# An S4D convolution block with a feed-forward: where the start of the kernel stores spectra, adds the skip weights and forms the modulation

## The chip, the cores and the metric

The kernel runs on one core of one Trainium2 chip. A core has TensorE (PE, with its weight loads PEld), VectorE (DVE), ScalarE (ACT), GpSimd (POOL) and SyncE (SP), which share an on-chip memory, and 16 DMA engines between that memory and DRAM. Every engine works through its own row of instructions in order; semaphores hold it back until what it reads is there. DMA transfers are issued by an engine (here SP, POOL and ACT) onto a queue of its own. The metric is the device time of one launch, in microseconds (us).

## The reference, cut to what matters

```python
def S4D(u):                                # u: (1, 2048, 576); D = 576 channels, N = 128 states
    dt = exp(log_dt);  A = -exp(log_A_real) + 1j * A_imag;  C = (C_real + 1j * C_imag) * dt
    K = 2 * einsum("dn,dnl->dl", C, exp(A * dt * pos)).real       # a kernel of 2048 taps a channel
    y = irfft(rfft(u, 4096) * rfft(K, 4096))[:2048]               # a causal convolution
    return y + u * D_skip
sa, ca, ga, sb, cb, gb = split(silu(c) @ w_mod, 6)                # modulation rows, 576 each
h = layernorm(x) * (1 + ca) + sa
x = x + ga * S4D(h)
h = layernorm(x) * (1 + cb) + sb
x = x + gb * (relu(h @ w1) @ w2)                                  # 576 -> 4608 -> 576
```

All inputs and the output are fp32. `y + u * D_skip` is the same as adding `D_skip` to tap 0 of each channel's kernel K, which is how both kernels do it.

## The kernel before

The 2048 rows are four blocks of 512. The S4D kernel has 2048 taps too, in four pieces; the convolution is done block against piece, in the frequency domain, with the transforms written as matmuls (`transform`, `transform1`, `inverse`) and sums and differences on DVE (`butterfly`). Block s needs the spectra U of blocks 0 to s and the spectra of the kernel pieces. `Ud` and `Rd` in DRAM keep such spectra for the later blocks. The channels go through in two halves, p = 0 and p = 1 (so U_0_0, K_0_1 and so on, the block first). The feed-forward of a block follows its convolution; the convolution of the next block, and the rest of the S4D kernel, are spread in small steps over the feed-forward ahead.

*The S4D kernel's first piece.* `KGen.first` makes it in six groups of 96 channels. A group consists of angles (`turns`: `ph` on PE from `zt` and `zr`, then fractions on DVE), exponentials and sines (ACT: `E`, `s`, `c`, `Zp`, `zs`), products of them on DVE and POOL (the factors `W1` and `W2`, each computed by doubling), and matmuls `kps <- W, W` that multiply the factors out (`products`). ACT copies a group's taps from PSUM to the table `ke` (`rows`, line 351); after three groups, that is half of the channels, `store` (line 446) writes `ke` to `kd` in DRAM with two DMAs, and `load_kt` reads it back in another layout as the tile `kt`, on SP's queue for block 0. The half 0 is stored at 110 us and loaded at 128, the half 1 at 176.6 and 179.7. `zs` are spectra of the generator (called `Zd` in DRAM, two stores a group, line 349) which the feed-forward loads back when it makes the rest of the kernel.

*Before the first group.* `KGen.setup` makes the rates: first `turn` and `rate` for parts[0], and then `turn` for the two other parts (ten DVE instructions with `ai`, `th`, `zt`), exponentials on ACT, and `rate` for them (`lar`, `zr`), then `cc`. `mod` makes the first three modulation rows: silu of `c` (ACT `ex`, DVE `ex`, its reciprocal, `ct`, and `cb`, the columns spread out), fifty matmuls for each row (`mod_products`), and the row's spreading over the partitions. The order of the `next(...)` calls in `KGen.first` (lines 377 to 395) is the order on the engines; nothing reorders it.

*From the last group to the feed-forward.* `first` stops inside the sixth group, and `main` runs the convolution of block 0 in the order of its generator: the transform of the kernel's half 0 (`mm_K(0)`, PE `ps_f` at 147.9), of the block's halves (`mm_U`), the last group's products (`late`) and `rows` with its store, the load of `kt` for half 1, the last three modulation rows (`mod_late`: the same matmuls for `sb`, `cb`, `gb`, two transposes each for `sb` and `cb`), the butterflies of U_0_0, U_0_1 and K_0_0 on DVE, and the transform of the kernel's half 1 (`transform1`, PE `ps_f` at 186.7). A save of a spectrum to DRAM (`save`, line 840) is a DMA issued by POOL, 1152 KB each.

*The skip weights* are added with `skip` (line 1258), on one partition and 288 elements of `kt`, after the load: for the half 0 on DVE (called in `early`, line 639), for the half 1 on POOL (called in `mm_K`). The skip weights lie in partition 0 of the tile `m_gb` and come with one DMA at the start.

Of the kernel before, what the change touches and what calls it, by code (L numbers as in the profile page):

```python
# [18 lines left out]
P = 128  # L19
# [4 lines left out]
NB = 4  # L24
NF = F // P
G = 96
# [23 lines left out]
class KGen:  # L50
# [31 lines left out]
    def setup(self, I):  # L82


        nc, pc = self.nc, self.pc
        kept = self.tc.keep_in_program_order
        tmp = lambda n: self.pw.tile([KR, NH, P], F32, tag="W2", bufs=5, name=n)
        lar, ai = tmp("lar"), tmp("ai")
        dtT = pc.tile([KR, NH], F32, name="dtT")
        lv = pc.tile([KR, NS], F32, name="lv")  # L90
        dt = self.pc.tile([P, D], F32, tag="T0", bufs=2, name="dt")
        self.cc = self.pa.tile([P, 2, D], F32, name="cc")
        self.halfpi = pc.tile([P, 1], F32, name="halfpi")
# [12 lines left out]
        z = self.zz = [self.pa.tile([KR, NH, P], F32R, name=f"z{n}") for n in "tr"]  # L106

        def split(zx, src, h):
            if h.start == 0:
                self.act(zx[:, h], src, AF.Copy)  # L110
            else:
                kept(nc.vector.tensor_copy(zx[:, h], src))
            self.v(zx[64:, h], src[64:], zx[64:, h], ALU.subtract)

        def turn(h):
            th = self.pc.tile([KR, 4, P], F32, tag="T1", bufs=2, name="th")
            dtb = dtT[:, h].unsqueeze(2).broadcast_to([KR, 4, P])
# [12 lines left out]
        self.diag(lv, slice(0, 8))  # L130
        turn(parts[0])
        self.diag(lv, slice(16, 25))
        self.diag(lv, slice(32, NS))
        yield
        rate(parts[0])
        yield
        self.diag(lv, slice(8, 16))
        self.diag(lv, slice(25, 32))
        yield
        for h in parts[1:]:  # L140
            turn(h)
        self.act(lar[:, 4:], lar[:, 4:], AF.Exp)
        self.act(dt, dt, AF.Exp)
        for h in parts[1:]:
            rate(h)
        for r in range(2):
            self.stt(
                self.cc[:, r], self.cc[:, r], 2.0 - 4.0 * r, dt, op0=ALU.mult, op1=ALU.mult
            )
        yield  # L150
# [111 lines left out]
    def powers(self, g, e, f):  # L262

        Z = self.ps.tile([P, 2, 512], F32, tag="Z", name=f"Zp_{g}")[:, :, 0 : 4 * G]
        Z = Z.rearrange("p r (i c) -> p r i c", c=G)
        zs = self.pc.tile([P, 2, 2, G], F32, tag="zs", bufs=2, name=f"zs_{g}")
        by_u = lambda x: x.rearrange("p i (u c) -> p u i c", u=2)
        c = self.abs(f)
        self.act(by_u(Z[:, 1]), f[:, :, 0:4], AF.Sin, scale=-TWO_PI)
        self.act(by_u(zs[:, :, 1]), f[:, :, 4:6], AF.Sin, scale=-TWO_PI)  # L270
        self.cos(by_u(Z[:, 0]), c[:, :, 0:4])
        self.cos(by_u(zs[:, :, 0]), c[:, :, 4:6])
        for r in (1, 0):
            self.pool(by_u(zs[:, :, r]), by_u(zs[:, :, r]), e[:, :, 4:6], op=ALU.mult)
        self.Z[g] = Z, zs

        def moduli():
            for r in (1, 0):
                self.v(by_u(Z[:, r]), by_u(Z[:, r]), e[:, :, 0:4], ALU.mult)

        return moduli
# [42 lines left out]
    def first(self, setup, mod):  # L324
# [8 lines left out]
        def sines(g):  # L333
# [12 lines left out]
            self.moduli = self.powers(g, E[4], F[2])  # L346
            zs = self.Z[g][1]
            for u in range(2):
                nc.sync.dma_start(out=k.Zd[2 * g + u], in_=zs[:, :, :, u * H : u * H + H])

        def rows(g):
            qs = slice(24 * (g % 3), 24 * (g % 3) + 24)
            self.act(ke[:, :, qs], ps[g].rearrange("p q a -> p a q"), AF.Copy)
            if g % 3 == 2:
                self.store(0, g // 3, ke.rearrange("p a q -> p (a q)"), nc.sync)

        def save(g):
# [26 lines left out]
        some(turns, 2)  # L384
        next(setup)
        run(turns, self.exps(0))
        next(mod)
        next(setup)
        next(mod)
# [182 lines left out]
class Body:  # L572
# [3 lines left out]
    def build(self):  # L576
        nc, tc, I = self.nc, self.tc, self.I
        with ExitStack() as ctx:
# [15 lines left out]
            self.x2, self.xT, self.ended = {}, {}, -1  # L594
            self.sm = self.pool(ctx, "sm")
            self.gb = self.sm.tile([P, D], F32, name="m_gb")
            self.dsk = self.gb[0:1]
            nc.gpsimd.dma_start(out=self.dsk, in_=I["dsk"].unsqueeze(0))
            self.x2p = [self.pool(ctx, "x2a")]
            kg = KGen(self)  # L600
            with ExitStack() as c2:
# [5 lines left out]
    def early(self, kg):  # L607
# [28 lines left out]
            ))  # L636
        yield
        self.kt0 = kg.kt0
        kept(self.skip(self.kt0, 0, nc.vector))
        for i in (0, 2, 1, 3):  # L640
            kept(nc.vector.tensor_tensor(h[:, i], h[:, i], self.m["ca"], op=ALU.mult))
            kept(nc.vector.tensor_tensor(h[:, i], h[:, i], self.m["sa"], op=ALU.add))
# [93 lines left out]
    def mod_late(self):  # L736


        nc, act, cb = self.nc, self.nc.scalar.activation, self.cb
        for j, nm in ((3, "sb"), (4, "cb"), (5, "gb")):  # L740
            self.mod_weights(self.wm[nm], slice(j * D, (j + 1) * D), nc.sync)
        for nm in ("sb", "cb", "gb"):
            yield
            w = self.wm[nm]
            ps = self.cps.tile([P, 512], F32, tag="cps", bufs=self.nps, name=f"mps_{nm}")
            self.mod_products(ps, cb, w, nc.tensor.matmul)
            row = self.cv.tile([P, 2 * P], F32, tag="row", bufs=1, name=f"row_{nm}")
            act(row[:, 0:P], ps[:, 0:P], AF.Copy)
            for o in (P, P + 64):
                act(row[0:32, o : o + 64], ps[0:32, P : P + 64], AF.Copy)  # L750
            if nm == "gb":
                yield
                self.mod_spread(row, self.md[nm], self.m[nm], Kept(self.tc, nc.gpsimd))
                return
            ps = self.cps.tile([P, 512], F32, tag="cps", bufs=self.nps, name=f"mpt_{nm}")
            nc.tensor.transpose(ps[:, 0:P], row[:, 0:P], self.ident)
            nc.tensor.transpose(ps[:, P : P + 32], row[0:32, P:], self.ident[:32, :32])
            act(
                self.m[nm], ps[:, 0 : 5 * 32].rearrange("p (j r) -> p j r", r=32)[:, :, 0],
                AF.Copy, bias=1.0 if nm == "cb" else 0.0,  # L760
            )

    def pool(self, ctx, name, **kw):
        return ctx.enter_context(
# [172 lines left out]
    def conv(self, s):  # L937
# [31 lines left out]

        def mm_K(p, Z):  # L970
            ktv = kt[p].rearrange("p (t dd g) q -> p t dd g q", t=2, g=2)
            if s == 0 and p == 1:
                self.skip(kt[p], p, Kept(self.tc, nc.gpsimd))
            src = lambda n2: ktv[:, n2 // 2, :, n2 % 2]
            if s == 0 and p == 1:
                return self.transform1(src, self.fcK, self.fcKn, Z)
            return self.transform(src, self.fcK, Z, s == 0)

        def spec_U(p, Z):
            U = self.spec(f"U_{s}_{p}")  # L980
            yield from self.butterfly(Z, U, -1)
            yield -1
            if s + 1 < NB or p == 1:
                self.save(self.Ud[s][p], U)
            Us.append(U if s == 0 or p == 0 else None)

# [86 lines left out]
        if s == 0:  # L1073
# [14 lines left out]
            yield from spec_K(0, ZK)  # L1088
            ZK = self.spec("Z")
            yield from mm_K(1, ZK)  # L1090
            self.save(self.Rd[0][0], Ks[0], Kept(self.tc, nc.gpsimd))
        else:
            yield from both(self.norm1(x2, h), mm_K(0, ZK))
            kt[1] = kernel_tile(1)
# [156 lines left out]
    def load_kt(self, kt, s, p, eng):  # L1251
# [2 lines left out]
            out=kt,  # L1254
            in_=bass.AP(tensor=kd.tensor, offset=kd.offset, ap=[[72, P], [9216, 16], [1, 72]]),
        )

    def skip(self, kt, p, eng):
        k0 = kt.rearrange("p (t dd g) q -> p t dd g q", t=2, g=2)[0:1, 0, :, 0]
        dv = self.dsk.rearrange("o (dd p q) -> o dd p q", dd=4, p=2)[:, :, p]  # L1260
        return eng.tensor_tensor(k0, k0, dv, op=ALU.add)

    def ffn(self, gens):

# [311 lines left out]
def _layout(inputs):  # L1576
# [14 lines left out]
    r["dsk"] = a["A_D_skip"]  # L1591
# [44 lines left out]
```

## Time and profile before

| | us |
|---|---|
| median of three runs | 1326.09 (1322.65, 1326.09, 1332.2) |
| the profiled execution | 1328.0 |
| its span, first to last instruction | 1326.2 |
| mean granted PE clock, as a share of full speed | 0.943 |

Busy over the whole span: PE 1212.6 us (91%), DVE 895.2 (67%), ACT 494.3 (37%), POOL 160.3 (12%). The feed-forward's first matmul comes at 228.7 us (`hps`, line 1330). The stretch ahead of it is what the change edits. There DVE is the engine with the most work.

| stretch, us | what runs | PE busy | DVE busy | PE clock | DMA GB/s |
|---|---|---|---|---|---|
| 0 to 23 | loads, first angles, first exponentials | 6.7 | 9.4 | 1.00 | 263 |
| 23 to 36 | turns, rates, first modulation rows | 9.1 | 12.4 | 1.00 | 230 |
| 36 to 140 | six groups of the kernel | 63.7 | 96.1 | 0.56 | 256 |
| 140 to 162 | transforms of kernel half 0 and of x | 16.2 | 21.7 | 0.77 | 302 |
| 162 to 187 | last group, its store and load, modulation | 14.9 | 23.9 | 0.73 | 313 |
| 187 to 229 | transform of half 1, product, inverse, norm | 30.7 | 32.9 | 0.84 | 142 |

Read such a table with the engines' waits beside it: an engine that is idle costs time only if the work that ends last stands behind it.

### The profile page before, as it was taken

To read this page: it belongs to the slowest core of one execution; us is meant where nothing else is said; L and a number is where in the kernel's file an instruction comes from. 1 tells how busy PE (TensorE), PEld (TensorE's weight loads), DVE (VectorE), ACT (ScalarE), POOL (GpSimd) and SP (SyncE) were. 2 spreads that over 40 slices of the span, in tenths; PEclk is the share of its full clock that TensorE was granted. 3 is DMA by queue.
4 is the path that set the end of the run, shared out by engine and by line. 5 is a ranking of instruction groups with operands and counts; after the bars stand their busy time and mean duration, and the time that the engine had idled before them with its cause. 6 is when DMAs were issued, how large, how long until landed. Compare 5 with 4: busy or idle time off the path is not lost.

```text
span 1326.2 us, 25994 instructions
## 1 busy us (share of the span) xinstructions
PE 1212.6 (91%) x10720; PEld 960.7 (72%) x10720; DVE 895.2 (67%) x1324; ACT 494.3 (37%) x863; POOL 160.3 (12%) x256
## 2 busy tenths in 40 slices
PE   4566676899989999999999999999999999999998
PEld 3344554677767787777777887887888888888886
DVE  5989988999986999689468994457996222111112
ACT  5677623222223422622243225433323353223231
POOL 0756511011000100100001000100000000000000
PEclk9556777999989999999999999999999999999999
DMA  8567882889878967799779995867996667666652
GB/s 273 210 235 294 300 314 80 345 298 333 311 259 302 342 223 278 247 403 343 262 270 339 351 340 159 285 205 285 346 395 189 173 177 230 195 202 191 200 178 70
DMA packets 122635, 345.85 MB, mean 261 GB/s; under 512 B 23916, under 2 KB 24212, under 8 KB 111764
## 3 DMA queue, kind: packets, MB, share of 16 engines
q1 hardware_dynamic: 105940, 228.14, 51.8%
q0 software_dynamic: 16064, 114.67, 23.0%
q8 instruction: 84, 1.38, 0.4%
q10 hardware_dynamic: 512, 1.38, 0.3%
q14 instruction: 35, 0.29, 0.1%
HBM read 262.73 MB, written 81.40 MB: 259 GB/s over the span
## 4 chain that ended last, share of the span: by engine, by line
PE 70%; DVE 17%; DMA 6%; issue 4%; ACT 2%; POOL 1%; SPq 0%; ACTq 0%; DVEq 0%; POOLq 0%
PE hps L1330 28%; PE acc L1356 28%; PE ps_f L850 5%; DMA L1d<-w 3%; PE kps L71 2%; PE ph L71 2%; DVE W1r L484 2%; DVE T L482 2%; PE ps_i L1057 2%; PE kps L517 1%; DVE w L1300 1%; DMA x<-in_x_dram 1%; DVE W1r L486 1%; DVE W1r L488 1%; DVE w L1312 1%
## 5 line engine op out<-in xcount | busy, mean ns | idle before, releaser
L1330 PE MATMUL hps<-xh,w 128*128 128x512 f32 x1152 | 395.7, 404 | 0.7 <-ACT xh L47 0.7
L1356 PE MATMUL acc<-w,hh 128*128 128x512 f32 x1136 | 362.1, 401 | 3.7 <-ACT hh L1335 3.5
L1336 DVE SCALAR_TENSOR_TENSOR hl<-hps,hh 128x512 fp32r<-128x512 f32 x144 | 99.4, 690 | 309.2 <-ACT hh L1335 308.5
L1330 PEld LDWEIGHTS hps<-xh,w 128*128 128x128 f32 x1152 | 219.0, 191 | 48.9 <-ACT xh L47 1.3
L1356 PEld LDWEIGHTS acc<-w,hh 128*128 128x128 f32 x1136 | 212.4, 188 | 50.3 <-ACT hh L1335 4.4
L1330 PE MATMUL hps<-xl,w 128*128 128x512 f32 x576 | 228.0, 397 | 0.1
L1356 PE MATMUL acc<-w,hl 128*128 128x512 f32 x568 | 219.8, 399 | 1.5 <-DVE hl L1336 1.5
L1335 ACT ACTIVATE hh<-hps 128x512 fp32r<-128x512 f32 x144 | 86.0, 597 | 329.9 <-PE hps L1330 325.2
L1305 ACT ACTIVATE w<-r 128x576 fp32r<-128x576 f32 x141 | 96.7, 686 | 225.3 <-PE acc L1356 224.9
L1330 PEld LDWEIGHTS hps<-xl,w 128*128 128x128 f32 x576 | 109.2, 190 | 23.5 <-DVE xl L47 0.6
L1356 PEld LDWEIGHTS acc<-w,hl 128*128 128x128 f32 x568 | 106.1, 188 | 25.4 <-DVE hl L1336 3.3
L1295 ACT ACTIVATE w<-r 128x640 fp32r<-128x640 f32 x140 | 102.5, 732 | 51.2 <-DMA L1d<-w 50.5
L1330 PE MATMUL hps<-xs,w 128*128 128x512 f32 x288 | 98.7, 412 | 0.0
L71 PE MATMUL kps<-W,W 128*32 128x16 f32 x2304 | 39.4, 210 | 45.8 <-POOL W L68 28.1
L1036 DVE TENSOR_TENSOR Y<-Y,T 128x1152 f32<-128x1152 f32 x60 | 79.5, 1353 | 0.0
L71 PEld LDWEIGHTS kps<-W,W 128*32 128x32 f32 x2304 | 34.6, 142 | 59.5 <-POOL W L68 31.2
L851 ACT ACTIVATE Z<-ps_f 128x288 f32<-128x288 f32 x120 | 48.9, 409 | 71.1 <-PE ps_f L850 69.3
L517 PEld LDWEIGHTS kps<-W1r,W2r 128*32 128x32 f32 x3456 | 45.1, 113 | 38.6 <-issue 19.2
L517 PE MATMUL kps<-W1r,W2r 128*32 128x48 f32 (+2 forms) x3456 | 52.4, 202 | 15.5 <-ACT ker L527 10.8
L1330 PEld LDWEIGHTS hps<-xs,w 128*128 128x128 f32 x288 | 53.8, 190 | 11.3
L1356 PE MATMUL acc<-hh,w 128*128 128x512 f32 x142 | 56.9, 401 | 0.0
L1356 PE MATMUL acc<-hl,w 128*128 128x512 f32 x142 | 56.1, 395 | 0.0
(249 smaller groups left out, 1547.1 us busy)
## 6 DMA issues: line engine op xcount, KB each, us to landing
r<-in_w_dram SPq DMA_DIRECT2D x144, 320.0 KB, 6.0
r<-in_w_dram SPq DMA_DIRECT2D x144, 288.0 KB, 3.7
w<-L1d SPq DMA_DIRECT2D x108, 320.0 KB, 4.2
w<-L2d SPq DMA_DIRECT2D x108, 288.0 KB, 2.6
W2r<-W2d POOLq DMA_DIRECT2D x18, 1536.0 KB, 9.0
W2d<-W SPq DMA_DIRECT2D x12, 1536.0 KB, 8.7
Ua<-Ud POOLq DMA_DIRECT2D x15, 1152.0 KB, 9.3
W<-W1d POOLq DMA_DIRECT2D x18, 768.0 KB, 9.5
```

Source lines behind the costliest of these rows:

```text
L71: self.tc.keep_in_program_order(self.nc.tensor.matmul(*args, **kw))
L482: v(T, X, zi, op=ALU.mult)
L517: nc.tensor.matmul(ps[32 * dd : 32 * dd + 32, q, :], W2[:, r, ch], W1[:, r, ch], start=(r == 0), stop=(r == 1),)
L850: nc.tensor.matmul(o, fc[:, n2, c, :], src(n2), start=True, stop=True)
L851: ev = nc.scalar.activation(Z[:, n2, c], ps[:, :PC], AF.Copy)
L1036: v(y, y, T, op=op or ALU.add)
L1295: copy(g - 1)(w1[g][:, 0], r1[g], AF.Copy)
L1305: copy(g)(w[:, 0:D], r2[g], AF.Copy)
L1330: nc.tensor.matmul(ps, a, x, start=(i == 0), stop=(i == 13))
L1335: nc.scalar.activation(hh, ps, AF.Relu)
L1336: nc.vector.scalar_tensor_tensor(hl, ps, 0.0, hh, op0=ALU.max, op1=ALU.subtract)
L1356: nc.tensor.matmul(acc[i], a, x, start=(f == 0 and seen[i] == 1), stop=(f == NF - 1 and seen[i] == (3 if i < 4 else 2)),)
```

## The change

The computation stays the same; five things are written otherwise.

1. *Spectra of the generator.* The tile `zs` has its two halves one behind the other, so a `Zd` store takes 768 bytes in a row from each of 128 partitions. Before, it was 512 pieces of 192 bytes. The scaling on POOL and the sines on ACT are the same in number and size.
2. *Skip weights.* They come in the layout of `ke`, prepared on the host side of the inputs, on a tile of their own (128x144), and POOL adds them to `ke` (128x72) after the third and the sixth group, between ACT's last copy and the store. `skip` and its two calls are gone.
3. *Spectra of x's first block.* The saves of U_0_0 and U_0_1 are called behind the transform of the kernel's half 1, next to that of K_0_0. Before, each came when its butterfly was done.
4. *Modulation rows of the second kind.* The products of `cb` come ahead of the transposes of `sb`, those of `gb` ahead of the transposes of `cb`; the row tile has two buffers. The weights are loaded in the order `sb`, `cb`, `gb`.
5. *First angles.* `setup` yields once more, so that the ten turn instructions come ahead of `mod`'s silu.

```diff
@@ setup
         for h in parts[1:]:
             turn(h)
+        yield
         self.act(lar[:, 4:], lar[:, 4:], AF.Exp)
@@ powers
-        zs = self.pc.tile([P, 2, 2, G], F32, tag="zs", bufs=2, name=f"zs_{g}")
+        zs = self.pc.tile([P, 2, 2, 2, H], F32, tag="zs", bufs=2, name=f"zs_{g}")
...
-            self.pool(by_u(zs[:, :, r]), by_u(zs[:, :, r]), e[:, :, 4:6], op=ALU.mult)
+            self.pool(zs[:, :, :, r], zs[:, :, :, r], e[:, :, 4:6], op=ALU.mult)
@@ first
-                nc.sync.dma_start(out=k.Zd[2 * g + u], in_=zs[:, :, :, u * H : u * H + H])
+                nc.sync.dma_start(out=k.Zd[2 * g + u], in_=zs[:, u].rearrange("p i r c -> p (i r c)"))
...
             if g % 3 == 2:
+                self.pool(ke[:, 0], ke[:, 0], k.dsk[:, g // 3], op=ALU.add)
                 self.store(0, g // 3, ke.rearrange("p a q -> p (a q)"), nc.sync)
...
         run(turns, self.exps(0))
+        next(setup)
         next(mod)
@@ early
-        kept(self.skip(self.kt0, 0, nc.vector))
@@ mod_late
+        yield
+        rows = {}
         for nm in ("sb", "cb", "gb"):
-            yield
...
-            row = self.cv.tile([P, 2 * P], F32, tag="row", bufs=1, name=f"row_{nm}")
+            row = rows[nm] = self.cv.tile([P, 2 * P], F32, tag="row", bufs=2, name=f"row_{nm}")
...
+            nm = {"cb": "sb", "gb": "cb"}.get(nm)
+            if nm:
+                row = rows[nm]
...
@@ main
-            if s == 0 and p == 1:
-                self.skip(kt[p], p, Kept(self.tc, nc.gpsimd))
...
-            if s + 1 < NB or p == 1:
+            if s and (s + 1 < NB or p == 1):
                 self.save(self.Ud[s][p], U)
...
             yield from mm_K(1, ZK)
-            self.save(self.Rd[0][0], Ks[0], Kept(self.tc, nc.gpsimd))
+            for dst, t in zip((*self.Ud[0], self.Rd[0][0]), (*Us, Ks[0])):
+                self.save(dst, t, Kept(self.tc, nc.gpsimd))
@@ inputs
+    r["dsk"] = np.zeros((4, 32, 2, 72), np.float32)
+    r["dsk"][:, 0] = a["A_D_skip"][perm].reshape(2, 6, 4, 12).transpose(2, 0, 1, 3).reshape(4, 2, 72)
```

DVE's row ahead of the first group, before. `ex`, `ct` and `cb` are the silu of c; `ai`, `th`, `zt` are turns:

```order
L62 TENSOR_TENSOR k_305<-ph_306,k_305 128x2x288
L679 TENSOR_SCALAR ex<-ex 128x5
L680 RECIPROCAL ex<-ex 128x5
L62 TENSOR_TENSOR ct<-ct,ex 128x5
L683 COPY cb<-ct 128x160
L62 TENSOR_TENSOR ai<-ai,dtT 112x512
```

And after, from the last three turn instructions on:

```order
L65 SCALAR_TENSOR_TENSOR th<-ai,th 112x512
L112 CAST zt<-th 112x512
L62 TENSOR_TENSOR zt<-th,zt 48x512
L681 TENSOR_SCALAR ex<-ex 128x5
L682 RECIPROCAL ex<-ex 128x5
L62 TENSOR_TENSOR ct<-ct,ex 128x5
L685 COPY cb<-ct 128x160
L65 SCALAR_TENSOR_TENSOR lar<-lar,dtT 112x512
```

The four instructions moved from ahead of the ten turns to behind them. The second place is POOL's row from the last group's factor products on, before:

```order
L68 TENSOR_TENSOR W_5_2048<-T_2236,T_2237 128x48x8 x2
L68 TENSOR_TENSOR W_5_2048<-T_2242,T_2243 128x48x8 x2
L841 DMA Ud_0_101<-U_0_2671 128x2304
L841 DMA Ud_1_102<-U_1_2684 128x2304
L47 TENSOR_TENSOR kt<-kt,m_gb 1x4x72
L47 DMA Rd_0_109<-K_0_2697 128x2304
L841 DMA Rd_1_110<-K_1_2762 128x2304
```

And after:

```order
L68 TENSOR_TENSOR W_5_2050<-T_2237,T_2238 128x48x8 x2
L68 TENSOR_TENSOR W_5_2050<-T_2243,T_2244 128x48x8 x2
L68 TENSOR_TENSOR ke_1609<-ke_1609,dsk 128x72
L47 DMA Ud_0_101<-U_0_2673 128x2304
L47 DMA Ud_1_102<-U_1_2685 128x2304
L47 DMA Rd_0_109<-K_0_2697 128x2304
L845 DMA Rd_1_110<-K_1_2763 128x2304
```

POOL now adds to `ke` ahead of all three saves, and nothing stands between them. The third place is PE's row from the last group's products to the transform of half 1, before:

```order
L731 MATMUL mps_sb<-wm_sb,cb 32x64 x5
L756 MATMUL mpt_sb<-ident,row_sb 128x128
L731 MATMUL mps_cb<-wm_cb,cb 32x128
L757 MATMUL mpt_sb<-ident,row_sb 128x32
L731 MATMUL mps_cb<-wm_cb,cb 32x128 x19
L731 MATMUL mps_cb<-wm_cb,cb 32x64 x5
L756 MATMUL mpt_cb<-ident,row_cb 128x128
L731 MATMUL mps_gb<-wm_gb,cb 32x128
L757 MATMUL mpt_cb<-ident,row_cb 128x32
L731 MATMUL mps_gb<-wm_gb,cb 32x128 x19
L731 MATMUL mps_gb<-wm_gb,cb 32x64 x5
L889 MATMUL ps_f<-kt,fcK 128x288
```

And after:

```order
L733 MATMUL mps_sb<-wm_sb,cb 32x128 x20
L733 MATMUL mps_sb<-wm_sb,cb 32x64 x5
L733 MATMUL mps_cb<-wm_cb,cb 32x128 x20
L733 MATMUL mps_cb<-wm_cb,cb 32x64 x5
L757 MATMUL mpt_sb<-ident,row_sb 128x128
L758 MATMUL mpt_sb<-ident,row_sb 128x32
L733 MATMUL mps_gb<-wm_gb,cb 32x128 x20
L733 MATMUL mps_gb<-wm_gb,cb 32x64 x5
L757 MATMUL mpt_cb<-ident,row_cb 128x128
L758 MATMUL mpt_cb<-ident,row_cb 128x32
L893 MATMUL ps_f<-kt,fcK 128x288
```

The transposes of a row (`mpt`) moved behind the next row's products, so PE has products to do while ACT copies the row.

More of the change, by code (lines that the diff above doesn't have):

```diff
@@ L269, in powers @@
         self.act(by_u(Z[:, 1]), f[:, :, 0:4], AF.Sin, scale=-TWO_PI)
-        self.act(by_u(zs[:, :, 1]), f[:, :, 4:6], AF.Sin, scale=-TWO_PI)
+        self.act(zs[:, :, :, 1], f[:, :, 4:6], AF.Sin, scale=-TWO_PI)
         self.cos(by_u(Z[:, 0]), c[:, :, 0:4])
-        self.cos(by_u(zs[:, :, 0]), c[:, :, 4:6])
+        self.cos(zs[:, :, :, 0], c[:, :, 4:6])
         for r in (1, 0):
-            self.pool(by_u(zs[:, :, r]), by_u(zs[:, :, r]), e[:, :, 4:6], op=ALU.mult)
+            self.pool(zs[:, :, :, r], zs[:, :, :, r], e[:, :, 4:6], op=ALU.mult)
         self.Z[g] = Z, zs
@@ L596, in build @@
             self.gb = self.sm.tile([P, D], F32, name="m_gb")
-            self.dsk = self.gb[0:1]
-            nc.gpsimd.dma_start(out=self.dsk, in_=I["dsk"].unsqueeze(0))
+            self.dsk = self.sm.tile([P, 2, 72], F32, name="dsk")
+            nc.gpsimd.dma_start(out=self.dsk, in_=I["dsk"])
             self.x2p = [self.pool(ctx, "x2a")]
@@ L741, in mod_late @@
             self.mod_weights(self.wm[nm], slice(j * D, (j + 1) * D), nc.sync)
+        yield
+        rows = {}
         for nm in ("sb", "cb", "gb"):
-            yield
-            w = self.wm[nm]
             ps = self.cps.tile([P, 512], F32, tag="cps", bufs=self.nps, name=f"mps_{nm}")
-            self.mod_products(ps, cb, w, nc.tensor.matmul)
-            row = self.cv.tile([P, 2 * P], F32, tag="row", bufs=1, name=f"row_{nm}")
+            self.mod_products(ps, cb, self.wm[nm], nc.tensor.matmul)
+            row = rows[nm] = self.cv.tile([P, 2 * P], F32, tag="row", bufs=2, name=f"row_{nm}")
             act(row[:, 0:P], ps[:, 0:P], AF.Copy)
@@ L750, in mod_late @@
                 act(row[0:32, o : o + 64], ps[0:32, P : P + 64], AF.Copy)
[L751 to L761, printed above, removed]
+            nm = {"cb": "sb", "gb": "cb"}.get(nm)
+            if nm:
+                row = rows[nm]
+                ps = self.cps.tile([P, 512], F32, tag="cps", bufs=self.nps, name=f"mpt_{nm}")
+                nc.tensor.transpose(ps[:, 0:P], row[:, 0:P], self.ident)
+                nc.tensor.transpose(ps[:, P : P + 32], row[0:32, P:], self.ident[:32, :32])
+                act(
+                    self.m[nm], ps[:, 0 : 5 * 32].rearrange("p (j r) -> p j r", r=32)[:, :, 0],
+                    AF.Copy, bias=1.0 if nm == "cb" else 0.0,
+                )
+            yield
+        self.mod_spread(rows["gb"], self.md["gb"], self.m["gb"], Kept(self.tc, nc.gpsimd))
+        yield
     def pool(self, ctx, name, **kw):
@@ L1256, in load_kt @@
         )
[L1258 to L1261, printed above, removed]
     def ffn(self, gens):
@@ L1590, in _layout @@
     r["lv"] = np.array(SLOTS, dtype=np.float32)
-    r["dsk"] = a["A_D_skip"]
+    r["dsk"] = np.zeros((4, 32, 2, 72), np.float32)
+    r["dsk"][:, 0] = a["A_D_skip"][perm].reshape(2, 6, 4, 12).transpose(2, 0, 1, 3).reshape(4, 2, 72)
+    r["dsk"] = r["dsk"].reshape(P, 2, 72)
     w1 = a["B_w1"]
```

## The prediction

> **What bounds the kernel now.** I read the page's span and its chain first, then the busy time by stretch, and only then the chain and the timeline of the stretches that the change touches.
>
> ```profile
> span 1326.2 us, 25994 instructions
> ...
> PE hps L1330 28%; PE acc L1356 28%; PE ps_f L850 5%; DMA L1d<-w 3%; PE kps L71 2%; PE ph L71 2%; DVE W1r L484 2%; DVE T L482 2%; PE ps_i L1057 2%; PE kps L517 1%; DVE w L1300 1%; DMA x<-in_x_dram 1%; DVE W1r L486 1%; DVE W1r L488 1%; DVE w L1312 1%
> ```
>
> ```profile
> 36.00:140.00 104.00, 63.70 (x1841) 46.63 (x1841) 96.06 (x211) 82.42 (x115) 70.72 (x99) 0.56 0.69 256
> ...
> 229.00:440.00 211.00, 195.87 (x2960) 151.66 (x2958) 188.38 (x228) 58.71 (x112) 21.85 (x39) 0.97 0.84 303
> 440.00:1326.00 886.00, 875.52 (x4897) 705.10 (x4896) 510.46 (x712) 305.87 (x543) 45.18 (x80) 1.00 0.75 255
> ```
>
> The second line is the chain that ended last by line: the two feed-forward matmuls, 28% each, lead it. The rows below it give, for a stretch, its length and then the busy time of PE, PEld, DVE, ACT and POOL. From 440 us on PE is busy 875.5 of 886 us, from 229 to 440 it is 195.9 of 211. The change edits nothing there, so a microsecond won before 229 us is a microsecond of the span, and the work behind only starts earlier. From 36 to 140 DVE is busy 96.1 of 104 us and PE 63.7: the six kernel groups are bound by DVE. So what counts ahead of 36 us is when DVE reaches the first group, and from 140 to 229 us the chain of waits.
>
> **The change, part by part.**
>
> *Conditioning behind the turns.* Rows of the timeline: start, duration, engine, line, operation, tiles, and in brackets the idle time ahead with its releaser.
>
> ```profile
> 22.27 0.21 ACT L59 ACTIVATE ex<-ct 128x5 f32<-128x5 f32 x1
> ...
> 22.51 0.17 DVE L679 TENSOR_SCALAR ex<-ex 128x5 f32<-128x5 f32 x1 [4.84 <-ACT ex L59]
> ...
> 23.14 0.32 DVE L683 COPY cb<-ct 128x160 f32<-128x160 f32 x1
> ...
> 23.38 0.68 DVE L62 TENSOR_TENSOR ai<-ai,dtT 112x512 f32<-112x512 f32 x1
> ...
> 27.30 3.13 PE L71 MATMUL mps_Z<-wm_ca,cb 128*32 128x128 f32 x50
> ...
> 28.83 0.69 DVE L62 TENSOR_TENSOR zt<-th,zt 48x512 fp32r<-48x512 f32 x1
> ...
> 33.33 1.43 DVE L65 SCALAR_TENSOR_TENSOR cc<-cc,dt 128x576 f32<-128x576 f32 x2
> ...
> 37.32 0.40 DVE L65 SCALAR_TENSOR_TENSOR row_ca<-mps_Z,row_ga 128x128 f32<-128x128 f32 x2
> ```
>
> DVE stands still for 4.84 us until ACT delivers `ex`, because four small instructions (`ex`, its reciprocal, `ct`, `cb`; 22.51 to 23.46) stand ahead of ten turn instructions (23.38 to 29.52, 6.1 us) whose inputs are there. Put behind them, the turns fill the hole from about 17.7 to 23.8 and the four find `ex` finished at 22.48. Rates, `cc` and the first group follow 4.84 us earlier. What gets later is `cb`: about 24.7 instead of 23.46, so the conditioning products end 1.2 later, those of `ca` at 31.6 instead of 30.43. Their reader `row_ca` would be due at 37.32-4.84=32.5: covered, by 0.9 us. The groups behind it are full of DVE work, so I keep all of it: **-4.84**, bounds 0 and -4.84.
>
> *Skip added to `ke` rather than `kt`, first half.* The chain of waits in the second stretch (start, us, what; "issue" is time in which an engine waits for nothing that the profile shows), and four rows of its timeline:
>
> ```profile
> 137.81 2.90 issue
> ...
> 142.12 2.04 issue
> 144.16 0.70 PE kps L71 x29
> ...
> 147.91 14.00 PE ps_f L850 x48
> 161.91 1.75 PE kps L71 x129
> 163.67 5.41 issue
> ...
> 171.02 3.70 issue
> 174.72 1.31 PE kps L71 x70
> ...
> 176.11 0.50 ACT ke L59
> ...
> 176.63 0.47 SPq L450
> ...
> 177.15 2.54 DMA kd<-ke
> ...
> 179.74 5.74 DMA kt<-kd
> ...
> 185.64 1.02 POOL kt L47
> ...
> 186.71 0.75 PE ps_f L889 x2
> ...
> 194.24 1.01 DVE K L47 x2
> ```
>
> ```profile
> 147.26 0.44 DVE L1261 TENSOR_TENSOR kt<-kt,m_gb 1x288 f32<-1x288 f32 x1
> ...
> 155.36 4.92 POOL L68 TENSOR_TENSOR W<-T,T 128x384 f32<-128x384 f32 x4 [8.40 <-DVE T L62]
> ...
> 183.24 2.76 DVE L47 TENSOR_TENSOR V<-Y 128x576 f32<-128x576 f32 x4
> ...
> 186.55 0.28 ACT L748 ACTIVATE row_gb<-mps_gb 128x128 f32<-128x128 f32 x1 [2.03 <-PE mps_gb L731]
> ```
>
> The first PE transform of the kernel (`ps_f`, 147.91) reads `kt`, on which DVE finishes the skip add of 0.44 us at 147.70, behind other DVE work. The kernel tile itself was fetched long before. Without that add PE may go on when the last of 29 `kps` ends, at 144.87: -3.0. POOL's four products for the last `kps` end at 160.28, the add's 0.44 earlier is 159.84, while `ps_f` would end at 158.9 and the first half of `kps` needs only the first two of the four; so nothing eats this but a tenth: **-2.9**. The other end is 0: the page calls the gap "issue", and if it is a fetch of code like the 2.90 and 2.04 ahead, it stays. DVE's end 0.2 us before PE's start is the nearer sign.
>
> *Two saves of U go later.* The last run of `kps`, from 161.91 on, pauses 5.41 and 3.70 us. Earlier in the same stream such pauses take 2.90 and 2.04. Between 9.11 and 4.94 I take half, **-2.1** (bounds 0 and -4.2): the saves of U leave this stretch, but the loads of modulation weights stay. So the last `kps` ends near 171.0 instead of 176.03.
>
> *Skip, second half.* Behind that `kps` comes a line of single steps: ACT `ke`, the store `kd`, the load `kt`, POOL's skip 1.02 us, transform. The skip goes (185.48 to 186.71, -1.2); in front of the store comes POOL's add of 128x72, which the trace lacks. Its nearest rows on POOL:
>
> ```profile
> L68 POOL TENSOR_TENSOR zs<-zs,E x6: 600/634/637, 106.3 to 145.3; 128x192 f32<-128x192 f32 x6
> ```
>
> 192 elements take 0.6 us, so 72 take between 0.2 (in proportion) and 0.6; I take 0.35, and 0.1 for the handover: **-0.7** in all. The same add for the first half of the kernel stands at 110 us ahead of a load that is not needed for 30 us: nothing. The modulation products must also be over before the transform; they ended at 186.5 and lose two waits of PE for ACT (0.8 us) by standing in a row, so they keep their 0.2 us of lead and give nothing themselves.
>
> *What is queued behind the new wait.* On POOL the saves of U0, U1 and of K0 now stand behind the `ke` add, and go out together just when `kd` and `kt` make their way. That is 3 x 1152 KB = 3.54 MB. Before, this stretch had the engines nearly to itself:
>
> ```profile
> 170.00:176.00 6.00, 2.30 (x163) 2.19 (x159) 6.00 (x11) 0.00 (x0) 0.53 (x1) 0.50 0.94 387
> 176.00:178.00 2.00, 2.00 (x44) 1.56 (x36) 2.00 (x3) 0.49 (x1) 0.00 (x0) 0.50 0.23 97
> 180.00:186.00 6.00, 5.52 (x101) 3.75 (x102) 5.93 (x7) 1.04 (x8) 0.36 (x1) 1.00 0.93 263
> ```
>
> ```profile
> Ud<-U POOLq DMA_DIRECT2D x7, 1152.0 KB, 8.0
> ...
> kd<-ker SPq DMA_DIRECT2D x12, 288.0 KB, 6.7
> kt<-kd POOLq DMA_DIRECT2D x6, 576.0 KB, 8.2
> ...
> Zd<-zs SPq DMA_DIRECT2D x12, 96.0 KB, 10.1
> ```
>
> The last two columns of the first rows are the DMA engines' busy share and GB/s: 0.94 at 387 before, 0.23 at 97 in the 2 us of the `kd` store. In the chain `kd` took 2.54 and `kt` 5.74; among the heavy traffic of the feed-forward the same two move in 6.7 and 8.2 (second rows, median to landing). So +4.2 and +2.5: **+6.6**. Bounds: 0 if the two still slip through, and +13.5 if all 3.54 MB go ahead of `kt` at the 263 GB/s that the last window shows. I take the loaded rows since they are the same two transfers beside the same kind of neighbours. A rule bears on this: the Trainium skill, "DMA: Bandwidth & Descriptors", section "Queues, rings and completion order", says that each DMA engine goes round its queues packet by packet. By it `kt`, in small pieces on SP's queue, would alternate with the big pieces on POOL's and land only when that backlog is through, so by it the upper bound would hold and the sum would be +3; no run here shows it yet.
>
> The waits on those saves themselves are covered: before, K0's save went out at 186.6 and the DVE product that reuses its tile started at 194.24; now it leaves some 13 us earlier, against at most 13.5 us of backlog. The first feed-forward weights stand on SP behind the issue of `kt`; they shift with `kd`, by 4.2, and their readers with the transform, by 6.6.
>
> *Spectra stores.* A `Zd` store is 128 pieces of 768 bytes instead of 512 of 192. It lands 10.1 us after issue and is read during the feed-forward: nothing on the path. POOL's scaling of `zs` keeps its size.
>
> **The sum.** -4.84-2.9-2.1-0.7+6.6 = -3.9. Span 1326.2-3.9 = 1322.3. The profiled execution took 1328.0, 1.8 over its span, and lies 1.9 above the median of the three runs, 1326.09; against that median the forecast is **1322**.
>
> **The rivals.**
> - *B, the saves slip past.* If `kd` and `kt` move as before, the gain is 4.84+2.9+2.1+0.7 = 10.5: 1315.6. For it speaks that the engines were at 0.23 in that stretch. Against it, that 3.54 MB need 9.1 us even at 387 GB/s. DVE would not stop it: its last `V` ended at 186.0, 8 us ahead of `K` at 194.24.
> - *C, slower: the backlog goes first.* POOL issues all three saves at once, and `kt` waits for their 3.54 MB: +13.5 instead of +6.6, so -10.5+13.5 = +3: 1329. It decides from 10.5 us of delay on. For it speaks the share of 0.93 at only 263 GB/s when `kt` itself moved. Against it, `kd` starts no later than the first save. The page named above, of the Trainium skill, speaks for this one; no trace here has the two queues meet in this way.
> - *D, nothing arrives.* The hole of 4.84 us does not pass through to the end of the groups (some wait of the first group on ACT or PE takes it up), while the rest goes as in the sum: -3.9+4.84 = +0.9: 1327. Against it stands the DVE share of 92% in the groups.
>
> **How the numbers follow.** My forecast (about 1322, its own range 1319 to 1325) gets 0.5; B 0.27; C 0.15; D 0.08. A measurement of this kernel can tell about 1% (13 us) from no change. More than 1% faster means under 1312.8, 2.8 us beyond B, which needs the whole 4.2 of the pauses and more: 0.1. More than 1% slower means over 1339, 10 us beyond C: 0.05. The rest, 0.85, is within 1%. The range goes from 1311 (B with pauses of 4.94, 2.1 us more, and 2 us of spread) to 1331 (C and 2 us).
>
> **What would show it.** Right, step by step: no idle time of DVE ahead of `ex`, `cc` at 28.5; `ps_f` starts within 0.3 us of the `kps` before it; pauses of `kps` that sum to 5 to 9 us; `kd` and `kt` at 6 to 8 us each where they had 2.54 and 5.74; the transform 16 to 17 us behind the last `kps`, where it was 10.7. Wrong: `kt` landing as fast as before (B), or the transform over 20 us behind the last `kps` (C), or the first group on DVE early but the sixth not (D).

## The result, and the profile after

| | before | changed |
|---|---|---|
| median of 11 runs, us | 1325.55 (1320.23 to 1332.2) | 1334.58 (1329.59 to 1337.81) |
| span of the profiled execution, us | 1326.2 | 1333.6 |

The ratio is 1.0058, 95% interval 1.0035 to 1.0080: slower by 7.7 us (4.6 to 10.6). The forecast was 1322 with a range up to 1331; the time lies above both.

The start of DVE's row in the changed kernel, from the timeline (start, duration, engine, line, operation, tiles, idle time ahead):

```profile
17.75 0.68 DVE L62 TENSOR_TENSOR ai<-ai,dtT 112x512 f32<-112x512 f32 x1
...
23.92 0.17 DVE L681 TENSOR_SCALAR ex<-ex 128x5 f32<-128x5 f32 x1
...
28.57 1.43 DVE L65 SCALAR_TENSOR_TENSOR cc<-cc,dt 128x576 f32<-128x576 f32 x2
```

No idle time stands ahead of DVE's `ex` any more; the turns begin at 17.75, and `cc` starts at 28.57 where it was 33.33, 4.76 sooner. So the first step went as forecast. The chain of waits from the first transform on:

```profile
149.82 5.09 PE ps_f L854 x20
154.91 1.75 PE kps L71 x125
156.66 5.85 issue
...
164.46 3.97 issue
...
169.82 0.50 ACT ke L59
...
170.39 5.11 POOL ke L68
...
176.04 7.48 DMA kd<-ke
...
183.58 6.72 DMA kt<-kd
...
190.43 1.30 PE ps_f L893 x2
191.73 0.96 PE ps_f L895 x2
...
194.61 0.74 PE ps_f L893 x2
195.35 0.48 PE ps_f L895 x2
...
200.20 1.01 DVE K L47 x2
...
203.10 1.27 DVE Y L47
```

Beside the chain of before, step by step (us from the start of each span):

| | before | changed | difference |
|---|---|---|---|
| `cc` starts | 33.33 | 28.57 | -4.8 |
| last run of `kps` starts | 161.91 | 154.91 | -7.0 |
| last `kps` over, ACT `ke` starts | 176.11 | 169.82 | -6.3 |
| store `kd` issued | 176.63 | 175.52 | -1.1 |
| load `kt` issued | 179.74 | 183.58 | +3.8 |
| transform of half 1 starts | 186.71 | 190.43 | +3.7 |
| butterfly of K_0_1 starts | 194.24 | 200.20 | +6.0 |
| first feed-forward matmul that the chain waits for | 228.69 | 234.38 | +5.7 |
| end of the span | 1326.2 | 1333.6 | +7.4 |

So 6.3 us were won up to the last `kps`, and 12.3 were lost in the 30 us behind it, in three places that the chain names: POOL's add to `ke` (5.11), the store `kd` (7.48 where it was 2.54) with the load `kt` (6.72, was 5.74), and the transform's first five pieces of 0.7 to 1.3 us where the later ones take 0.48; the skip on `kt`, 1.0 us, is gone. The last 1.7 us come in the feed-forward, in one execution of each kernel; no part of the change was tied to them. (The matmul at 228.69 is the one on the chain. The feed-forward's very first `hps` came at 223.6 before and comes at 229.2 now.)

### The profile page after: what moved, and what is told of

It is laid out like the page before. It is cut to its first block, busy times and chain, and to the rows that moved or that the text cites. A ratio compares the mean times of both kernels' runs of the same rounds, so it can differ in the third digit from the quotient of the medians.

```text
span 1333.6 us, 25994 instructions
## 1 busy us (share of the span) xinstructions
PE 1212.9 (91%) x10720; PEld 959.8 (72%) x10720; DVE 894.5 (67%) x1323; ACT 495.3 (37%) x863; POOL 165.1 (12%) x257
## 4 chain that ended last, share of the span: by engine, by line
PE 71%; DVE 10%; DMA 5%; issue 2%; ACT 1%; POOL 0%; SPq 0%; DVEq 0%; ACTq 0%
PE hps L1328 30%; PE acc L1354 30%; PE ps_f L854 4%; PE kps L520 3%; DMA L1d<-w 2%; PE ps_i L1059 2%; DMA x<-in_x_dram 1%; DVE Y L1038 1%; DVE T L485 1%; DMA Ua<-Ud 1%; DVE T L1036 1%; DVE w L1298 1%; DVE W1r L487 1%; PE ps_t L1155 1%; DMA kd<-ke 1%
```

## The experiments

All were timed in 5 rounds against runs of the kernel before on the same chip. Ratios are to those runs, with 95% intervals; the changed kernel stands at 1.0058 (1.0035 to 1.0080).

**1. DVE pauses until the add is over.**

```diff
                 self.pool(ke[:, 0], ke[:, 0], k.dsk[:, g // 3], op=ALU.add)
+                if g > 3:
+                    Kept(k.tc, nc.gpsimd).memset(k.gt[:, 0:1], 0.0)
...
             yield from spec_K(0, ZK)
+            Kept(self.tc, nc.vector).tensor_copy(self.gt[:, 1:2], self.gt[:, 0:1])
```

> The changed kernel, but POOL writes one column of a scratch tile behind its add to ke, and DVE copies that column between the butterfly of K_0_0 and the first product, so DVE pauses until the add is over. Theory L (DVE's unbroken row of products with two on-chip inputs holds POOL back; the add of 5.10 us is waiting, not work): the add ends within 0.5 us of the butterfly's end, so it is 1.3 to 1.8 us long instead of 5.10, the store of kd is issued 3.3 to 3.8 us sooner after the last kps, and the time falls by about 3.5 to 1331. Rival R (the 5.10 us are POOL's own, a slow start after 14 idle us or code that has to come in): the add stays at about 5.1 us, DVE stands at the gate until then, the time stays at 1334.6.

Measured: 1.0011 (0.9995 to 1.0027). Against the changed kernel that is 0.47% less, about 6 us, with some 4 us of uncertainty. First POOL and DVE in the changed kernel, from its timeline:

```profile
168.60 2.89 DVE L47 TENSOR_TENSOR K<-W 128x576 f32<-128x576 f32 x6
...
170.39 5.10 POOL L68 TENSOR_TENSOR ke<-ke,dsk 128x72 f32<-128x72 f32 x1 [13.97 <-ACT ke L59]
...
171.41 2.62 DVE L47 TENSOR_TENSOR Y<-K,U 128x1152 f32<-128x1152 f32 x2
...
173.95 1.35 DVE L47 TENSOR_TENSOR T<-K,U 128x1152 f32<-128x1152 f32 x1
...
175.33 1.38 DVE L47 TENSOR_TENSOR Y<-Y,T 128x1152 f32<-128x1152 f32 x1
```

and the same place with the gate:

```profile
168.66 2.89 DVE L47 TENSOR_TENSOR K<-W 128x576 f32<-128x576 f32 x6
...
170.18 1.56 POOL L68 TENSOR_TENSOR ke<-ke,dsk 128x72 f32<-128x72 f32 x1 [13.71 <-ACT ke L59]
...
171.81 0.15 DVE L47 COPY gt<-gt 128x1 f32<-128x1 f32 x1 [0.26 <-POOL gt L47]
171.88 2.62 DVE L47 TENSOR_TENSOR Y<-K,U 128x1152 f32<-128x1152 f32 x2
```

The same add of 128x72 takes 5.10 us in the one and 1.56 in the other, and 0.34 for the half 0 at 105.8 us of the changed kernel. With the gate it is over 0.2 us after DVE's butterfly (168.66+2.89=171.55). Without it, the add ends at 175.49, 0.16 us after the start of the first DVE instruction (`Y<-Y,T`) that reads what the one ahead of it wrote. The instructions ahead of that one overlap: 171.41 starts before 168.60+2.89=171.49. In the kernel of experiment 6 below POOL starts elsewhere in the same row:

```profile
175.15 3.13 POOL L68 TENSOR_TENSOR ke<-ke,dsk 128x72 f32<-128x72 f32 x1 [16.61 <-ACT ke L59]
...
178.12 1.38 DVE L47 TENSOR_TENSOR Y<-Y,T 128x1152 f32<-128x1152 f32 x1
```

There the add took 3.13 us and ended at 178.28, again 0.16 after the start of `Y<-Y,T`. Theory L holds: most of the 5.10 us are a wait for the first break in DVE's row. Rival R falls. (`kd` and `kt` still take 7.67 and 7.21 us with the gate, so the saves are a loss of their own.) The Trainium skill, "SBUF — State Buffer", section "SBUF: two separate sides", says that DVE and GpSimd share a pair of ports, that a DVE operation with two on-chip inputs and a GpSimd operation that reads that memory exclude each other, and that the loser waits for the whole instruction. The trace agrees, with one addition: here the loser waited for a whole row of overlapping instructions and not for one.

**2. The saves wait until `kt` has landed.**

```diff
             yield from mm_K(1, ZK)
+            Kept(self.tc, nc.gpsimd).tensor_copy(self.gt[0:1, 0:1], kt[1][0:1, 0, 0:1])
             for dst, t in zip((*self.Ud[0], self.Rd[0][0]), (*Us, Ks[0])):
                 self.save(dst, t, Kept(self.tc, nc.gpsimd))
```

> The changed kernel, but POOL reads one element of kt ahead of the saves of U_0_0, U_0_1 and K_0_0, so that all three go out when kt has landed. Theory Q (the 3.5 MB of saves, issued 0.1 us ahead of kd, hold up kd and kt): kd takes 2.5 to 3 us instead of 7.48, kt 5.7 to 6 instead of 6.72, the transform starts 5 to 6 us sooner, the time falls by 5 to 8 to about 1328; the add to ke stays at about 5.1. Rival (kd is slow because of the other traffic, weights and W1d): kd and kt stay over 6 us, the time stays at 1334.6. If the saves, now later, hold up the second product, DVE waits ahead of K_0_1 and up to 4 us of the gain come back.

Measured: 1.0015 (0.9995 to 1.0035), 0.43% below the changed kernel. Its chain of waits:

```profile
170.20 5.10 POOL ke L68
...
175.84 2.55 DMA kd<-ke
...
178.44 4.32 DMA kt<-kd
...
184.14 15.03 DMA Rd<-K
...
199.26 1.36 DVE Y L47
```

The add still takes 5.10. `kd` falls from 7.48 to 2.55 and `kt` from 6.72 to 4.32, so theory Q holds, and `kd` bore most of it. The last two rows are the cost of saving late that the expectation named, at the next place: the save of K_0_0, third in its queue, lands 15.03 us after its issue, and DVE waits for that ahead of `Y`, at 199.26 where the changed kernel has 203.10. Of the 7.3 us won on `kd` and `kt`, 3.8 arrive.

**3. The half 1 skip back on `kt`.** The add to `ke` is done for g = 2 only, and the old `skip` call on POOL stands ahead of the three saves, which therefore wait for `kt`.

```diff
             if g % 3 == 2:
-                self.pool(ke[:, 0], ke[:, 0], k.dsk[:, g // 3], op=ALU.add)
+                if g < 3:
+                    self.pool(ke[:, 0], ke[:, 0], k.dsk[:, g // 3], op=ALU.add)
...
+            if s == 0 and p == 1:
+                self.skip(kt[p], p, Kept(self.tc, nc.gpsimd))
```

> The changed kernel, but the skip weights of the half 1 are added to kt on POOL as before (those of the half 0 stay in ke). That takes the add out from in front of the kd store, and the saves, behind the skip on POOL, wait for kt. Theories L and Q together: kd issued 5.1 us sooner after the last kps, kd and kt at 2.5 and 5.7 us, skip 1.2 us back: -5.1-5.9+1.2 = about -10, the time about 1325. If only Q holds: -5 to 1330. If neither: 1334 to 1336.

Measured: 0.9968 (0.9950 to 0.9987), 0.9% or 12 us below the changed kernel. (Its POOL row then has the skip, 1.26 us, and the saves.) The chain:

```profile
167.87 0.50 ACT ke L59
...
168.91 2.67 DMA kd<-ke
...
171.63 4.37 DMA kt<-kd
...
178.47 13.75 DMA Rd<-K
...
192.31 1.36 DVE Y L47
```

L and Q together, as expected: the store follows ACT's copy after 0.5 us, `kd` takes 2.67 and `kt` 4.37. `Y` starts at 192.31, 10.8 before the changed kernel's; 1.9 of it came before the last `kps`, which varies by 2 us from one profile to the next. The save of K_0_0 again lands late (13.75).

**4. The conditioning move alone**, on the kernel before (the two `yield` and `next(setup)` lines of the diff).

> The kernel before with only the conditioning moved behind the turns. If the hole of 4.84 us in DVE is worth what reaches the sixth group in the changed kernel: -4.0, about 1321.5. Rival D (it is taken up on the way): 1325.5, no change.

Measured: 0.9973 (0.9955 to 0.9991), -3.6 us (-6.0 to -1.2). The step is real, and rival D falls.

**5. The half 0 skip alone**, on the kernel before: POOL adds to `ke` at g = 2, and the DVE `skip` on `kt` is gone.

> The kernel before with only the half 0 skip moved from kt (DVE) to ke (POOL). Step of the prediction: the first transform starts 3.0 sooner after its kps and the time falls by 2.9. Rival (the second half of the transforms waits for DVE's scaling of h, which does not come sooner): the first transform starts 3 sooner, the last kps 0.5 to 1 sooner, and the time falls by at most 1.

Measured: 1.0004 (0.9984 to 1.0025): nothing. Its chain:

```profile
143.20 0.66 PE kps L71 x31
143.86 14.55 PE ps_f L853 x48
...
173.35 3.03 PE mps_sb L734 x44
176.38 1.40 issue
...
184.55 3.23 PE mps_gb L734 x48
187.78 0.68 PE ps_f L892 x2
```

The first transform does start right behind its `kps` (143.20+0.66), where before a gap of 3.0 us lay, and the last `kps` is over at 173.35, 2.7 sooner. But the modulation products now end last, and the transform waits for them: they take 14.4 us (173.35 to 187.78), where before they took 10.4 and were over 0.2 us before the skip. There is a pause of 1.40 us in them, and the granted clock (the third value from the end) is low for most of the time from 180 to 187, where before it was 1.00 from 180 to 186; so the last set of 48 products takes 3.23 us, where before one took 2.2:

```profile
180.00:188.00 8.00, 7.57 (x91) 4.66 (x82) 5.88 (x6) 0.78 (x5) 1.37 (x2) 0.57 1.05 327
```

At their old 10.4 us the products would have been over at 183.8, ahead of POOL's skip on `kt`, which ends at 185.32 here; the transform could then have started some 1.3 us sooner than before. The other part of the 2.7 us went into the store and the load of `kt`: POOL's skip started 11.1 us after the last `kps` (184.48) instead of 9.6 (185.64). The time excludes a gain of 2.9 us and allows the rival's gain of up to 1, but the last `kps` came 2.7 sooner and not the rival's 0.5 to 1. That the other executions lost the time in the same places isn't shown; there is one profile.

**6. Extra traffic beside the fifth group's `kps`.** Four DRAM to DRAM copies on SP's queue, none of them read.

```diff
                 k.load_kt(self.kt0, 0, 0, nc.sync)
+                for i in range(4):
+                    nc.sync.dma_start(out=k.junk[i], in_=k.W2d[i])
```

> The changed kernel with four extra DRAM to DRAM copies of 1536 KB on SP's queue, one of which falls at about 134 us beside the fifth group's kps. There the kps pause 3.08 and 1.50 us in the changed kernel. Theory of the prediction (a pause is PE's wait for its next instructions, and these come slower when the DMA engines are full): the pauses there rise to 4 us and more each; the last group's pauses (5.85 and 3.97), which the removed saves of U did not shorten, stay, since the stores and weight loads still fill the engines there. Rival (the long pauses of the last group have another cause than full DMA engines): the pauses at 134 to 141 stay below 3.3 and 2.3.

Measured: 1.0068 (1.0042 to 1.0095). The copy beside the fifth group was issued at 137.2 and moves from about 137.7 on, so both pauses met it:

```profile
137.61 2.73 issue
...
141.75 4.80 issue
```

```profile
137.60:140.34 2.74, 0.01 (x1) 0.00 (x0) 2.50 (x8) 1.96 (x4) 2.74 (x4) 0.85 1.57 558
141.75:146.50 4.75, 0.00 (x0) 0.00 (x0) 4.61 (x13) 1.59 (x3) 4.75 (x9) 0.51 0.90 348
```

The columns that count are the last two, DMA share and GB/s; a packet counts whole in the stretch where it starts, so a share can exceed 1. The second pause is 4.80, where the changed kernel has 1.50. But the first is 2.73, where the changed kernel has 3.08, and the engines were full there too. The last group's first pause stayed, as expected (5.68), and its second, which should have stayed as well, fell from 3.97 to 2.33; the DMA share was 0.16 there, against 0.61 in the changed kernel. So at the second place of each pair the pause was short where the engines were mostly idle, but full engines don't make every pause long.

What the prediction had wrong is that the saves of U fill the engines here. In the changed kernel they are full without them, since the stores and weight loads were there all the time:

```profile
150.00:165.00 15.00, 8.61 (x322) 7.07 (x321) 15.00 (x22) 4.14 (x11) 4.93 (x4) 0.86 1.05 339
```

A share of 1.05 in that stretch is the place of the first long pause (156.66 to 162.51). And the place of the saves of U doesn't move the pauses: they are 5.84 and 3.97 with the saves late (experiment 3) and 5.87 and 3.98 with the saves early (experiment 9).

That a pause is a wait for instructions, the DMA packets of the trace do bear out. The queue that the profile calls `q8 instruction` carries one packet of 16 KB in each of these pauses, or just ahead of it, and PE goes on 1.3 to 1.5 us after it is through: in the changed kernel these packets end at 135.79, 139.40, 161.03 and 167.05, and PE goes on at 137.24, 140.70, 162.51 and 168.43; the four of experiment 6 fit too. Such a packet itself takes 0.9 to 1.3 us each time. What differs is when it starts: in experiment 6, 0.4 us into the pause of 2.73 and 2.4 us into that of 4.80; in the changed kernel, 3.2 us into that of 5.85. Why it starts late stays open.

**7. The spectra layout and the modulation in a row**, on the kernel before.

> The kernel before with only the spectra layout and the modulation products in a row (both were costed at nothing). If that is right: within 1 us of before. Rival: the smaller number of packets (4608 fewer) frees the DMA engines in the stretch of 140 to 176 us and the pauses of kps shorten: 1 to 3 us less than before.

Measured: 0.9984 (0.9965 to 1.0004): -2.1 us, with zero just inside. The costing at nothing isn't refuted, a gain of 1 to 3 neither. The rival's way to it doesn't show: the last group's pauses are 5.41 and 3.97, against 5.41 and 3.70 before.

**8. Four more sets of products on PE**, so that it doesn't stand still ahead of the transform. Nothing reads them.

> The changed kernel with four more sets of modulation products on PE behind the last ones (about 9 us of PE work that nothing reads), so that PE does not stand still for 12.7 us ahead of the transform of half 1. Theory W (the granted PE clock falls to half while PE is idle, and the first five or so of the transform's matmul groups run at 0.96 instead of 0.48 us): the transform runs at 0.48 from its first or second group, 2 us less than the changed kernel. Rival (the transform is slow at first for want of something else, such as its code): 0.96 for the first groups as before, no change.

Measured: 1.0096 (1.0065 to 1.0126). The first groups ran at 0.96 as before, which is the rival's answer, but the run doesn't decide: all but 14 of the 200 extra products were over 4.4 us before `kt` landed, and the granted clock fell again in those 4.4 us. (The last 14 ran inside the transform, for 1.1 us.) It also cost some 5 us against the changed kernel, with as much uncertainty, 1.9 of them in `kd` (9.41). What theory W rests on is a comparison of rows of the others. In the changed kernel PE stands still for 12.7 us ahead of the transform, in experiment 3 for 1.4. The changed kernel first:

```profile
185.00:190.40 5.40, 0.00 (x0) 0.00 (x0) 0.00 (x0) 0.00 (x0) 0.00 (x0) 0.50 1.07 278
190.40:195.00 4.60, 4.57 (x10) 3.31 (x11) 2.38 (x4) 2.70 (x5) 0.00 (x0) 0.50 1.05 391
195.00:200.00 5.00, 5.00 (x22) 3.94 (x21) 0.00 (x1) 1.95 (x6) 0.00 (x0) 1.00 0.90 302
```

and experiment 3:

```profile
177.00:182.00 5.00, 4.51 (x19) 3.57 (x20) 4.60 (x7) 3.23 (x7) 2.00 (x4) 1.00 1.05 402
```

The third value from the end of a row, ahead of DMA share and GB/s, is the granted clock: 0.50 while PE stands still and through the first 4.6 us of the transform, then 1.00; 1.00 from the start in experiment 3, where the pieces take 0.48 from the second on. Priced from the chain, the time from the transform's start to that of K_0_1 goes from 7.5 us before to 9.8, so it costs 2.2. The other kernels agree: with PE idle for 4.4 to 12.7 us ahead of it, the transform starts at half clock in all five (the changed kernel, experiments 1, 2, 6 and 8); with 1.4 us or less it starts at full clock in all seven (before, experiments 3, 4, 5, 7, 9 and 10). That the slow groups run at half the granted clock is read from the rows; that the idle time is what lowers it is argued from this comparison, and length alone isn't the rule: in experiment 5 the clock fell to half at about 180 us, soon after a pause of 1.4 us among the products, with PE busy.

**9. The half 1 skip on `kt`, and the saves of U at their old place.** Experiment 3 with the condition in `spec_U` and the single save of K_0_0 as before the change.

> The changed kernel with the skip weights of the half 1 on kt (POOL, as before), and with the saves of U_0_0 and U_0_1 back behind their butterflies; only that of K_0_0 waits for the skip. So it has the conditioning move, the half 0 skip in ke, the spectra layout and the modulation in a row. If the wait of DVE for the saves' landing (4.1 us ahead of Y_0_1 and 3.7 ahead of K_0_1 where all three saves went out behind kt) was the price of saving late: no such wait, and 3 to 7 us less than with the saves late, 8 to 11 less than before, about 1317. If instead early saves lengthen the pauses of kps by as much: the same as with the saves late, 4 less than before.

Measured: 0.9956 (0.9934 to 0.9978), -5.8 us (-8.8 to -2.9). It beats both kernels. It isn't told apart from experiment 3 (0.9968). Neither answer of the expectation names the reason: the early saves of U don't lengthen the pauses (5.87 and 3.98), but DVE still waits 4.6 us, for the save of K_0_0 ahead of K_0_1's butterfly, since that save stands behind the skip. On the path that wait is worth less: the transform starts at 181.05 and takes 7.5 us up to K_0_1 at full clock, so without the save K_0_1 could have started at about 188.6 instead of 189.8.

**10. As 9, with the save of K_0_0 ahead of the skip.**

> As the run with the half 1 skip on kt and the early saves of U, but the save of K_0_0 goes ahead of the skip on POOL, so it leaves at its butterfly's end, about 173, beside kd and kt, and not behind them. There DVE waited 4.6 us for that save's landing ahead of K_0_1. If that wait was on the path: it is gone, kd and kt take 1 to 3 us more together, and the time is 1 to 4 us less, about 8 below before. Rival (one save beside kd and kt costs as much as the wait): the same as that run, 6 below before.

Measured: 0.9963 (0.9939 to 0.9988), the same as 9. The chain:

```profile
170.99 4.43 DMA kd<-ke
...
175.48 5.24 DMA kt<-kd
...
180.89 1.36 POOL kt L47
...
189.83 1.01 DVE K L47 x2
```

DVE's wait for the save is gone, but `kd` and `kt` take 4.43 and 5.24 beside it (3.81 and 4.37 in 9). The trace goes with the rival: one save beside the two costs about as much as the wait behind them. The times alone, with some 4 us of uncertainty between 9 and 10, couldn't tell a gain of 1 to 4 us from none.

## Why the prediction was wrong, point by point

- *Conditioning, -4.84:* right. The trace shows -4.76 at `cc`, the run alone -3.6 (-6.0 to -1.2).
- *POOL's add to `ke`, 0.35:* the step that failed. I priced an operation by its size, from a row (`zs`) where DVE left gaps, and it waited 5.10 us for DVE. My upper end of 0.6 was no bound, since the row named did not have DVE's unbroken butterflies and products beside it. With the wait cut to the end of the butterfly (experiment 1) the add took 1.56.
- *Saves beside `kd` and `kt`, +6.6:* right in size: +4.9 and +1.0 measured, 5.9 in all, where I had split it +4.2 and +2.5. In mechanism it was case C that came, smaller than priced. In the changed kernel's trace the packets of the three saves go out from 176.57 to 187.50 us, and of the 2048 packets of `kt` none starts before 187.32, though its load was issued at 183.58:

```profile
q0 software_dynamic: 144, 1.18, 97.4%
...
q1 hardware_dynamic: 2175, 0.87, 118.0%
```

The first row is POOL's queue from 183.6 to 187.3 us, where no other queue starts a packet; the second is SP's, with `kt` on it, from 187.3 to 190.3 (packets, MB, share of the engines). `kd`, in pieces of 4608 bytes, had gone nearly one for one with the saves' pieces of 9216: 55 against 64 from 181 to 183 us. The rule of the Trainium skill's page "DMA: Bandwidth & Descriptors", section "Queues, rings and completion order", that an engine goes round its queues packet by packet, fits what `kd` did. `kt` came when the backlog was through, as I had drawn from that rule, but without taking turns before that; why is not shown. What I had wrong was the price: +13.5 puts the whole backlog on top of the 8.3 us that `kd` and `kt` take without it, but the backlog took 10.9 us and ran beside them. That the loaded rows came within 0.7 us of the total is in part luck. The transform came 20.6 us behind the last `kps`, past the 20 that I had given as the sign of C, but 4.8 of these are the add's.
- *Pauses of `kps`, -2.1:* wrong in sign: 5.85 and 3.97, 9.82 in all, against 9.11. The saves of U were not what made them long: early or late, the pauses are the same (experiments 9 and 3).
- *Half 0 skip, -2.9:* the transform started 3.0 sooner behind its `kps`, as said. In the changed kernel PE then waited for DVE's `h` at 149.82, so the last run of `kps` came 7.0 sooner, not 7.7; alone it was worth nothing (experiment 5); in its profile the modulation products, in part at half clock, became the last to end.
- *Layout and products in a row, 0 and nothing:* not refuted.
- *Left out:* the granted clock. The longer wait for `kt` leaves PE idle, and the transform begins at half clock, 2.2 us. That the one brings the other is argued from a comparison of kernels (experiment 8).

From the sum of -3.9 to the +6.0 at K_0_1: add +4.8, pauses +2.8 (0.7 lost, not 2.1 won), clock +2.2, the rest (transforms and groups less early than said, the two DMA steps 0.7 better than said) near nothing. 4.8+2.8+2.2=9.8, against 9.9. The kernel became slower not by what it moves onto the queue alone, which I had priced, but by that and the add together: with either undone (1 and 2) it stands 0.11 and 0.15% above before, with both undone (3) it is faster.

## What to carry to other kernels

Price a small operation on GpSimd by what VectorE does at that place, not by its size: on a critical path, beside a long row of VectorE operations with two on-chip inputs, it may wait for the first break in the row, an instruction that reads what the one ahead of it wrote. Before saves are moved "later", look at which short transfers on the critical path they will meet there, and at who reuses the saved tiles; here `kd` and `kt` lost 5.9 us beside the saves, and with the saves behind them DVE's wait took back 3.5 of the 7.3 us won. And a term that takes a wait away is worth only the lead of the next work to end, which needs a price of its own.

## What the runs showed of the hardware that was not expected

The POOL add of 128x72 took 0.34, 1.56, 3.13 and 5.10 us, the same shape in each case; the last three ended 0.2 us or less after the first break in DVE's row. In the other direction, POOL's skip on `kt` met DVE's four `V<-Y` operations in experiment 3, and these took 3.36 us instead of 2.77. Idle times of PE of 4.4 to 12.7 us ahead of the transform were followed by 3 to 5.5 us at half the granted clock; with 1.4 us or less ahead of it there was none, but a pause of 1.4 us among the products of experiment 5 was followed by half clock too. Each of PE's pauses in the fifth and sixth group's `kps` ended 1.3 to 1.5 us after a 16 KB packet on the instruction queue was through, in the changed kernel and in experiment 6. And 2048 packets of 288 bytes for `kt` didn't start until the last of 384 save packets of 9216 bytes had started.
